# Linear attention, then a GELU network, on one core: the first tile's attention in three units instead of two, and other instructions for r u k and for the state chain

## The chip, the cores and the metric

The kernel runs on one core of one Trainium2 chip. The metric is device microseconds for one execution. Before the change it was 582.84 us, the median of three runs (582.12 to 584.59).

## What is computed

The reference has two stages. Per batch entry and head, a state of 48 x 48 is carried over 768 tokens:

```python
cur = np.einsum('bhd,bhe->bhde', u[None] * kt, vt)
y[:, :, t] = np.einsum('bhd,bhde->bhe', rt, state + cur)
state = wt[:, :, :, None] * state + np.einsum('bhd,bhe->bhde', kt, vt)
```

r, k, v and w are of shape 4 x 8 x 768 x 48. Then y, as x of 3072 tokens by 384, goes through a network of width 2048:

```python
h = x @ w_in
g = 0.5 * h * (1.0 + erf(h * inv_sqrt2))
return (g @ w_out).astype(np.float32)
```

## The kernel before, in words

Tokens are cut into eight tiles of T = 384, two to a batch entry. For each tile there is an `attention` and an `mlp`. The eight heads are four pairs; a pair's two heads lie on the two halves of the 128 partitions. Within a tile tokens stand in chunks of C = 64, two chunks to a block of 128 tokens, so a pair of heads has three blocks (N3) and six chunks (NC).

The attention of a tile goes as follows. `tot` (L508) holds products of w over 2, 4, ... 64 neighbouring tokens. For the first two tiles `halves()` (L567) does, for h = 1, 2, 4, 8, 16, 32, one product d of r and k in each chunk (L550), then multiplies r and k by the decay across half blocks (L592, L603), then copies the part of d that belongs to this h into `a_sb`: by masked copies on VectorE (L615) up to h = 8, by ScalarE (L612) at 16 and 32. At h = 1 the diagonal with u comes too: ScalarE makes r times u (L497), TensorE the product with k, VectorE the masked copy (L563). For later tiles `quarters()` does the same in two levels, and the finest level by sums; it begins with r u k in one VectorE instruction per head pair (L487, four to a tile). Then k is transposed (kt, L787, or moved by DMAs in later tiles), `kv_ps` holds k v of each chunk (L817), `chain_states` (L829, L833) runs state = tot state + kv over the chunks, one `scalar_tensor_tensor` for each head pair and chunk, with kv read where TensorE wrote it, in PSUM. `inside()` (L848) is y from `a_sb`, and L906 adds what the states give. y is copied into `xT`, 384 rows as three groups of 128 (j): ScalarE or VectorE for the rows of the first three pairs (L913, L929), and the fourth pair through `ysb` and six small DMAs (L932, L936).

The network of the first tile is plain (`h_plain` L1114, `g_plain`): for each f of 16 a product over j of `w_in` and 384 columns of xT (L1121), Gelu by ScalarE (L1124), then o = g w_out (L1133). Later tiles do the products with fewer multiplications by sums made on VectorE (`h_ops`, `g_ops`; their products are all recorded at L1043), in an order written out by hand in `ORDER`.

The weights arrive as 64-bit numbers in 16 pieces of 768 KB (eight of w_in, which serve two f each, and eight of w_out). ScalarE (L432, L433, L435) and VectorE (L440, L443) convert each; SP issues the loads (L299, L304).

What fixes the order of instructions is `PLAN`: for each x one string in which each letter advances one generator by one step. For x = 0 the letters are the two units of the first tile's attention ("." for head pairs 0 and 1, "s" for 2 and 3), "f" the next tile's attention, "c" weight conversion, "l" loads, "x" warm products that compute nothing (`keep_warm`, L324; sixteen of them open the kernel, and each product of the first tile's attention but h = 1 has two behind it). For x = 1 and later "." is the network of tile x - 1, "s" the attention of tile x, "f" the beginning of that of tile x + 1. All engines take their instructions in the order so made; a wait holds up all that stands behind it on that engine.

TensorE records two products for each f32 product that the program issues (96 records at L1121 are 48 instructions); transposes of kt record one.

Of the kernel before, what the change touches and what calls it, by code (L numbers as in the profile page):

```python
# [10 lines left out]
F32 = mybir.dt.float32  # L11
# [10 lines left out]
C = 64  # L22
# [18 lines left out]
        ".lls.....sslsc.lsslll.sl.sls..sl.lscsl..sss.lscs.lscs.s.clll.s..s.cccsss...wss..ss.ff"  # L41
    ),
    1: (
        "c.ccc.clccs.cc..csscc...wcsc.csc.s.c.ccsc.scl..c..csclwccs.ccc.sc.cccs..ccs.c..csss.c...s.ccss.scl.l"
        "wccc..ll.csccl.ccclcc.cfc.cwfwf..wcw.sfff...ff.w....lww.fff.fsfx.xfx..w.w.....w.f..f.cw.f..xx.."
    ),
    2: (
        "ss.w.s.sswssw.s.s....s...slsl.s.s.sw..ww.ss.w..sw...sw.ss..w......swws.ss..s.s..s.sss.l.wsw..s..ss.."
        ".s..l....ls.w..sw..s...w.s....ss.ssww.s..w.s...s.s.s..s.sl.s.......s.s.l........s..ls.s......s...l.."
        "f...ls...f..ff....fx.xx....ff.xffx"  # L50
    ),
    3: (
        ".................l...l...ss..s..ss...s.lsss..s..sss.s.s.sss..s..s.s.s......s.ss.ss.ss..s..ss.sss..ss"
        ".ss.s....l.sl..ss.....s.......ss.s.s..ss..s.s.ss..s.s...s......s.s...l....ssss..l..s.s.l..s.ls.f...f"
        "......lfxx.xx..x"
    ),
    4: (
        ".s.ss.l.......s.s............s....sl..s....sssss..s.ss..ss..s..ss......s.s..ssss..ss.sl..s..s..s.s.s"
        "s.s.....s.ss.ssss..ss.s.lss..ss.s..s.....s.s.l.s.s......sss.....ss.....ss..s...s.ssl..s..s...llsls.f"
        "....s.....f.l..fxx.xxx"  # L60
    ),
    5: (
        "...ss..ss.s..ss....s..s................l..ss.l.....s.slss.ss...s.ss.s....ss.s..s...sssss.sss..ss..s."
        "s....s...ssss.sss..s...ssss....s....ssss...s....sls.sssss..s..s........l.....s.....s..ssls..sl..ls.l"
        ".sf....f.f.f...lxxxx.x."
    ),
    6: (
        "...s...s.s.ss.s...s............l.s.....s...ss...ss....s.ss.s..ss..ssslss...s.s...ss.s.s...l.s.sl..ss"
        "s.s...s.s.ss..ss.s.s.sss..s.s...ss..s.ssss..sss...l..s...s.s..ss.s..........s....sl......ss.ls.l.lfs"
        ".s.ff.f....f..l..xx.xfffffffxx"  # L70
    ),
    7: (
        "........................s.s....sssss.s......sss.ss...ss.s...ssss..ss..s.s...ss.ss.....s..s.ss.s..s.s"
        "ss.s...s....s..s......s.s......s.....s..ss.ssss..s.ssss...s........s..s.s.s.s.s....s.......xx....xxx"
# [25 lines left out]
        "E0 e0 A0 a0 C0 c0 F0 B0 A1 b0 a1 E1 B1 F1 f0 e1 f1 k0 G0 G1 b1 g0 D0 A2 d0 a2 C1 l0 B2 g1 i0 c1 E2 e2 F2 "  # L100
        "C2 D1 j0 b2 l1 c2 d1 A3 k1 f2 G2 a3 g2 j1 k2 l2 i1 E3 e3 F3 f3 D2 C3 +22 c3 G3 g3 B3 =a +e5 D3 d2 <i l3 "
        "b3 d3 <g j3 j2 k3 i2 i3 +23 +03 +e0 =i =b +e1 =g =j +01 +e2 =k !b !k !g +e3 !a +E2 +E3 =h !j =c =m !h "
        "+00 =q !m +20 !c <p +E0 +e4 !q =l +E4 =n !l !n =s =p =o !s !p =f =t !f !o =r !t =d =e !r !d !i !e"
    ),
    2: (
        "A0 E0 a0 B0 F0 e0 b0 C0 A1 f0 a1 c0 G0 B1 g0 F1 E1 b1 f1 D0 e1 k0 C1 d0 !i c1 A2 a2 k1 G1 A3 i1 B2 g1 l0 "
        "b2 F2 i0 f2 D1 d1 a3 !b G2 j0 E2 l1 F3 B3 e2 C2 g2 b3 l2 c2 E3 j1 f3 G3 e3 C3 +22 g3 +e5 D2 l3 k2 j3 c3 "
        "d2 D3 i2 d3 =b j2 <g =a <i k3 +03 =g i3 =k =i +e0 +01 +00 +23 !k =j +e1 +e3 +20 !g =h !j +e2 +E3 +E2 =c "
        "!h !d =m +e4 !m !c =q <p +E0 =p =l !p !q =n !l +E4 !n =s !s =f =o !f =t =r !o !t =d =e !r !e !a"
    ),  # L110
    3: (
        "A0 E0 a0 B0 e0 b0 C0 A1 c0 F0 E1 a1 e1 f0 B1 b1 G0 A2 F1 g0 D0 C1 k0 l0 d0 f1 c1 a2 G1 F2 E2 g1 B2 k1 e2 "
        "D1 !a b2 f2 E3 d1 C2 e3 j0 c2 l1 A3 G2 a3 F3 j1 C3 k2 g2 !b i0 f3 D2 l2 d2 G3 g3 i1 D3 c3 k3 B3 <i l3 "
        "+22 d3 j3 b3 i3 j2 <g =i =a =g !d =b +03 =k i2 +23 +e0 +e5 !g +01 +e1 +e2 =j +e3 =h +E3 =c !k !h !j +00 "
        "!i +E2 =m +20 +E0 !m =q =l !q +e4 +E4 !l !c =n =s <p =p !s !p !n =o !o =f =t !f =r =d !t !r =e !e"
    ),
    4: (
        "A0 E0 a0 B0 e0 F0 b0 C0 f0 A1 G0 c0 E1 k0 a1 B1 g0 F1 e1 D0 b1 A2 l0 f1 C1 G1 d0 a2 g1 l1 B2 c1 b2 E2 D1 "
        "e2 F2 A3 f2 C2 j0 j1 d1 c2 a3 k1 k2 G2 F3 g2 i0 E3 f3 D2 i2 B3 e3 G3 l2 i1 g3 D3 d2 C3 b3 +22 <i l3 +e5 "
        "j2 j3 +e2 c3 d3 =i <g =b +03 +23 =g =a =k k3 !g =j +e0 i3 =h !d !k !j +01 !a =c +e1 +E2 +e3 +E3 !i +00 "  # L120
        "!h =m +20 !c !m +e4 =q <p !q =l +E0 !l +E4 =p =n =s !n !p !s =o !o !b =f =d !f =t =r !t !r =e !e"
    ),
    5: (
        "A0 E0 a0 F0 e0 B0 C0 b0 A1 f0 a1 G0 F1 g0 l0 f1 B1 c0 E1 e1 G1 b1 D0 C1 g1 k0 d0 A2 a2 c1 D1 !b E2 d1 B2 "
        "b2 l1 i0 F2 e2 C2 j0 k1 i1 c2 f2 A3 a3 G2 k2 F3 E3 g2 f3 D2 G3 d2 e3 l2 g3 j1 C3 i2 c3 B3 D3 +22 <i l3 "
        "!i k3 d3 =b <g j3 j2 +03 =g b3 +23 =i +e0 i3 !a =a +e5 +01 !g =k =h =j +e1 !k !j +e3 !h =c +e2 +E3 +E2 "
        "=m =q !c +00 !m !d +20 !q =l <p +e4 !l +E0 =p =n +E4 !p =s !n =o !s !o =t =f !f =d !t =r =e !r !e"
    ),
    6: (
        "A0 a0 E0 e0 F0 B0 C0 b0 A1 f0 G0 a1 c0 E1 B1 e1 k0 F1 C1 f1 c1 b1 G1 g0 k1 E2 A2 !a D0 d0 e2 g1 C2 l0 a2 "  # L130
        "c2 D1 d1 B2 A3 l1 b2 a3 F2 E3 f2 F3 !i j1 G2 i1 g2 B3 j0 f3 e3 !d i0 +22 D2 b3 l2 G3 +e5 +e2 k2 !b i2 g3 "
        "C3 D3 c3 l3 j3 d3 d2 <g =a =b j2 =g <i k3 +23 +03 +e0 i3 !g =k +01 =h +00 +E2 !k +e4 =i =c =j +e1 +E4 "
        "+20 !h =q +E0 !j +e3 +E3 !q !c =m !m <p =l =p !l =n =s !p !s !n =o =f !o !f =t !t =r =d =e !r !e"
# [15 lines left out]
def kernel(  # L149
# [72 lines left out]
    def units_of(x):  # L222
        return NPART if x == 0 else 1
# [14 lines left out]
    def load_first():  # L238

        t = bufs[0]  # L240
        loaded[0] = [None, None]
        size = 3 * NP * T // units_of(0)
        order = [(0, 2), (0, 0), (0, 1), (1, 2), (1, 0), (1, 1)]
        for n, (i, part) in enumerate(order):
            s = slice(i * size + part * size // 3, i * size + (part + 1) * size // 3)
            nc.sync.dma_start(out=t[:, s], in_=rkw[0, :, s])
            if n == 0:
                nc.sync.dma_start(out=u_sb, in_=u)
# [14 lines left out]
    def load(x, dma):  # L263

        if x >= NX:
            return
        loaded[x] = [None, None]
        for i in (0, 2, 1):
            t = bufs[x % 2 if i == 0 else 1]
            assert i == 0 or (x - 1, i) in behind, (x, i)  # L270
            for j in range(3):
                a = i * ALL + j * ALL // 3
                dma.dma_start(out=t[:, a:a + ALL // 3], in_=rkw[x, :, a:a + ALL // 3])
                if (i, j) == (1, 2):
                    behind.add((x, "in"))
                yield
        load_v(x, dma)
        yield
# [99 lines left out]
    def make_fine():  # L378
        nc.vector.tensor_tensor(out=fine_mask, in0=s_qs[FINE], in1=t_block, op=ALU.is_equal)
# [68 lines left out]
    def attention(x, unit):  # L448

        first = x % HALVES == 0  # L450
        parts = range(NPART) if units_of(x) == 1 else range(unit, unit + 1)
# [3 lines left out]
        n_u = qs * T  # L455
        base = unit * 3 * n_u
        r, k, w = (bufs[0 if x == 0 or i == 0 and x % 2 == 0 else 1][:, base + i * n_u:base + (i + 1) * n_u]
                   for i in range(3))
        rc, kc = (z.rearrange("p (b i c t) -> p b i c t", b=np_, c=2, t=C) for z in (r, k))
        at = a_sb[:, :, parts[0] * NI:(parts[0] + np_) * NI]  # L460
        st = st_bufs[x % 2]
        before = None if first else st_bufs[(x - 1) % 2]
# [20 lines left out]
        if x >= 2:  # L483
            assert (x - 1, "kx") in behind and (x, "in") in behind
            for q in range(qs):
                m_q = slice(q * T // FINE, (q + 1) * T // FINE)
                nc.vector.scalar_tensor_tensor(out=kx[:, 0:n_u].rearrange("p (a m) -> p m a", a=FINE)[:, m_q],  # L487
                                               in0=r4[:, m_q], scalar=u_sb[:, q:q + 1], in1=k4[:, m_q],
                                               op0=ALU.mult, op1=ALU.mult)
# [3 lines left out]
        else:  # L493

            rus = [kx[:, b * Q * T:(b + 1) * Q * T] for b in parts]
            for q in range(qs):
                nc.scalar.activation(out=rus[q // Q][:, q % Q * T:(q % Q + 1) * T], in_=r[:, q * T:(q + 1) * T], func=AF.Copy,  # L497
                                     scale=u_sb[:, q0 + q:q0 + q + 1])
            rucs = [ru.rearrange("p (i c t) -> p i c t", c=2, t=C) for ru in rus]
# [43 lines left out]
        def products(bs, right, width, rest=False):  # L543
# [10 lines left out]
            if x == 0 and not rest:  # L554
                keep_warm(2)
# [766 lines left out]
```

## Time and profile before

| what | value |
|---|---|
| median of three runs | 582.84 us (582.12 to 584.59) |
| the profiled execution | 583.43 us, its span 581.7 us |
| TensorE busy (PE), weight loads (PEld) | 567.2 us (98%), 510.4 us (88%) |
| VectorE (DVE), ScalarE (ACT) busy | 453.0 us (78%), 290.2 us (50%) |
| warm products, L324 | 46 recorded, 14.7 us |
| first h product, L1121 | starts at 46.26 us |
| first product of the second tile's network | near 125.8 us |
| TensorE clock granted, mean | 0.997 |

The page gives busy time per engine and then the span in 40 equal slices, one digit each, in tenths. A row of the table by stretch reads: the stretch, its length, then busy time and number of instructions of PE, PEld, DVE, ACT and POOL, the granted clock, the share of DMA engines busy and GB/s. The chain of work that ended last is a list of start, length and what it was; "issue" is time in which an engine waited for nothing that the profile shows. A group of instructions reads: line, engine, operation, output<-input, shapes, count, then busy us and mean ns of one, then idle time of the engine just before and who ended it. The mean of one instruction can be longer than its step, since neighbours overlap.

### The profile page before, as it was taken

To read this page: it belongs to the slowest core of one execution; us is meant where nothing else is said; L and a number is where in the kernel's file an instruction comes from. 1 tells how busy PE (TensorE), PEld (TensorE's weight loads), DVE (VectorE), ACT (ScalarE), POOL (GpSimd) and SP (SyncE) were. 2 spreads that over 40 slices of the span, in tenths; PEclk is the share of its full clock that TensorE was granted. 3 is DMA by queue.
4 is the path that set the end of the run, shared out by engine and by line. 5 is a ranking of instruction groups with operands and counts; after the bars stand their busy time and mean duration, and the time that the engine had idled before them with its cause. 6 is when DMAs were issued, how large, how long until landed. Compare 5 with 4: busy or idle time off the path is not lost.

```text
span 581.7 us, 17597 instructions
## 1 busy us (share of the span) xinstructions
PE 567.2 (98%) x7544; PEld 510.4 (88%) x7544; DVE 453.0 (78%) x880; ACT 290.2 (50%) x634; POOL 58.8 (10%) x63
## 2 busy tenths in 40 slices
PE   7789999999999999999999999999999999999997
PEld 3476666669999999999999999999999999999997
DVE  6878967989889978688887979789788988730171
ACT  2468987134762358235672357324671357425520
POOL 3100000003100030003100120003100021002200
PEclk9999999999999999999999999999999999999999
DMA  6669833222451442345223631526314242212401
GB/s 241 200 193 334 275 111 110 70 79 37 68 130 54 112 85 41 95 127 93 29 39 99 171 43 15 126 70 163 43 28 106 94 56 29 43 39 42 54 1 41
DMA packets 61853, 55.07 MB, mean 95 GB/s; under 512 B 32336, under 2 KB 46928, under 8 KB 61776
## 3 DMA queue, kind: packets, MB, share of 16 engines
q1 hardware_dynamic: 50256, 45.62, 26.1%
q0 software_dynamic: 11424, 8.26, 10.9%
q8 instruction: 59, 0.97, 0.7%
q14 instruction: 18, 0.15, 0.1%
q10 hardware_dynamic: 96, 0.07, 0.0%
HBM read 36.24 MB, written 4.72 MB: 70 GB/s over the span
## 4 chain that ended last, share of the span: by engine, by line
PE 94%; DVE 2%; DMA 1%; issue 1%; ACT 0%; SPq 0%; DVEq 0%
PE u_ps L1043 33%; PE h_ps L1043 19%; PE o_ps L1043 13%; PE h_ps L1121 6%; PE o_ps L1133 5%; PE d L689 5%; PE d L550 4%; PE kv_ps L817 2%; PE y_ps L906 2%; PE y_ps L859 2%; DMA rkw<-in_rkw_dram 1%; PE warm L324 1%; DVE st L833 1%; PE d L680 1%; DVE kx L487 1%
## 5 line engine op out<-in xcount | busy, mean ns | idle before, releaser
L1043 PE MATMUL h_ps<-xT,w_in_sb 128*128 128x192 f32 x560 | 109.7, 328 | 0.0
L1081 POOL DMA_DIRECT2D g<-o_sb x42 | 50.8, 1268 | 477.6 <-ACT o_sb L1076 296.9
L1043 PEld LDWEIGHTS h_ps<-xT,w_in_sb 128*128 128x128 f32 x560 | 93.3, 190 | 2.1 <-ACT u_ps L1091 0.8
L1043 PE MATMUL u_ps<-w_out_sb,g 128*128 128x192 f32 x224 | 41.8, 330 | 0.3 <-DVE g L1157 0.3
L1043 PE MATMUL u_ps<-s,w_in_sb 128*128 128x192 f32 x224 | 41.3, 328 | 0.0
L705 ACT COPY a_sb<-d 32x320 f32<-32x320 f32 (+5 forms) x108 | 39.1, 362 | 3.5 <-PE d L689 1.7
L1043 PE MATMUL o_ps<-t,g 128*128 128x192 f32 x224 | 40.0, 326 | 0.0
L1043 PEld LDWEIGHTS u_ps<-w_out_sb,g 128*128 128x128 f32 x224 | 36.7, 190 | 1.0 <-issue 0.5
L1043 PEld LDWEIGHTS u_ps<-s,w_in_sb 128*128 128x128 f32 x224 | 36.9, 190 | 0.6
L1043 PEld LDWEIGHTS o_ps<-t,g 128*128 128x128 f32 x224 | 37.0, 190 | 0.0
L1188 ACT ACTIVATE o_sb<-u_ps 128x192 f32<-128x192 f32 x21 | 6.9, 331 | 57.6 <-PE u_ps L1043 57.5
L833 DVE SCALAR_TENSOR_TENSOR st<-st,tot_sb,kv_ps 128x48 f32<-128x48 f32 x160 | 29.5, 259 | 7.7 <-PE kv_ps L817 7.7
L723 DVE COPY_PREDICATED a_sb<-quarter,d 128x480 f32<-128x480 uint8 (+5 forms) x54 | 23.2, 438 | 13.1 <-PE d L689 12.0
L1121 PE MATMUL h_ps<-xT,w_in_sb 128*128 128x384 f32 x96 | 33.2, 494 | 0.0
L1133 PE MATMUL o_ps<-w_out_sb,g 128*128 128x384 f32 x96 | 31.8, 489 | 0.0
L550 PEld LDWEIGHTS d<-rkw 64*64 64x64 f32 x1152 | 20.2, 140 | 12.9 <-issue 8.3
L1043 PE MATMUL u_ps<-w_extra,g 128*128 128x192 f32 x168 | 30.9, 328 | 0.3 <-ACT u_ps L1167 0.3
L1072 ACT ACTIVATE g<-g 128x384 f32<-128x384 f32 x56 | 28.2, 522 | 5.9 <-DMA g<-o_sb 3.9
L1091 ACT COPY u_ps<-h_ps 128x384 f32<-128x384 f32 x28 | 13.1, 468 | 35.8 <-PE h_ps L1043 25.1
L1157 DVE TENSOR_TENSOR g<-g 128x512 f32<-128x512 f32 x42 | 28.1, 682 | 3.4 <-ACT g L1072 3.1
L689 PE MATMUL d<-kx,rkw 64*64 64x96 f32 x1152 | 29.9, 247 | 0.0
L1083 DVE TENSOR_TENSOR g<-g,o_sb 128x384 f32<-128x384 f32 x14 | 7.5, 548 | 28.4 <-ACT o_sb L1076 28.4
(163 smaller groups left out, 1211.1 us busy)
## 6 DMA issues: line engine op xcount, KB each, us to landing
rkw<-in_rkw_dram SPq DMA_DIRECT2D x54, 256.0 KB, 3.5
g<-o_sb POOLq DMA_DIRECT2D x42, 192.0 KB, 3.6
raw<-in_w_out_dram SPq DMA_DIRECT2D x8, 768.0 KB, 7.7
v_in<-in_v_dram SPq DMA_DIRECT2D x8, 584.0 KB, 4.5
raw<-in_w_in_dram SPq DMA_DIRECT2D x5, 768.0 KB, 5.7
rkw<-kx SPq DMA_DIRECT2D x72, 48.0 KB, 2.0
out_dram<-o_sb SPq DMA_DIRECT2D x17, 192.0 KB, 1.9
rkw<-in_rkw_dram SPq DMA_DIRECT2D x6, 384.0 KB, 3.5
```

What stands on the lines that cost most here:

```text
L550: nc.tensor.matmul(d[half[p], g, n * width:(n + 1) * width], lhsT=kc[half[g], b, i, p], rhs=right(half[g], b, i, p), start=True, stop=True)
L689: nc.tensor.matmul(o[half[p], i * 3 * C // 2:(i + 1) * 3 * C // 2], lhsT=kc[half[g], n // NI, n % NI, p], rhs=rx[half[g], 2 * n + p], star ...
L705: nc.scalar.copy(out=at[z, g, first:behind, (a + 1) * h:], in_=d[z, :, :, to] if g == slice(None) else d[z, :, to])
L723: nc.vector.copy_predicated(out=an[:, :, :, :, (a + 1) * h:], mask=mask.to_broadcast(data.shape), data=data)
L833: nc.vector.scalar_tensor_tensor(out=stq[:, q, c], in0=stq[:, q, c - 1] if c else b4[:, q, NC - 1], scalar=totq[:, q, c:c + 1], in1=kvs[q ...
L1043: nc.tensor.matmul(o, lhsT=lhsT, rhs=rhs, start=start, stop=True, skip_group_check=True)
L1072: nc.scalar.activation(out=g_of(q, a, b), in_=z, func=AF.Gelu)
L1081: nc.gpsimd.dma_start(out=o, in_=z, accum_op=ALU.add)
L1091: nc.scalar.copy(out=u_of[q], in_=a_of[q])
L1121: nc.tensor.matmul(h_ps, lhsT=w_in_sb[:, f // FI, j, f % FI * 128:(f % FI + 1) * 128], rhs=xT[:, j, :], start=(j == 0), stop=(j == NJ - 1))
L1133: nc.tensor.matmul(o, lhsT=gs[f // FG][:, f % FG, i * 128:(i + 1) * 128], rhs=w_out_sb[:, f, :], start=(f == 0), stop=(f == NF - 1))
L1157: (nc.vector.tensor_add if op == "+" else nc.vector.tensor_sub)(*(a(i) for i in (z if z != "E0" else "20", x_, y_)))
```

## The change

The first tile's attention becomes three units: unit 0 is head pairs 0 and 1 on tokens 0 to 255, unit 1 is pairs 2 and 3 on the same tokens, unit 2 is all four pairs on tokens 256 to 383 and goes on from their states. Each has 4 blocks, where the two units of before had 6. The loads of the first tile are cut to match (nine shares of 256 KB where six of 384 KB were), the third unit's shares come later, and unit 2 ("b") stands in the plan of x = 1, beside the first tile's network. There h is done first for 256 columns of xT, two f to a bank and a Gelu of 512 elements, and then for 128 columns, four f to a bank. o is as before.

```diff
-    def units_of(x):
-        return NPART if x == 0 else 1
+    UNITS = ((range(1), 0, 2), (range(1, 2), 0, 2), (range(NPART), 2, N3))
...
-                for f in range(group * FG, (group + 1) * FG):
-                    h_ps = bank("h_ps")[:, 0:T]
...
+            for lo, hi, units in ((0, a, (0, 1)), (a, z, (2,))):
+                assert all((0, "unit", unit) in behind for unit in units)
+                n = hi - lo
+                m = BANK // n
+                for f in range(0, NF, m):
+                    h_ps = bank("h_ps")
+                    for i in range(m):
+                        for j in range(NJ):
+                            nc.tensor.matmul(h_ps[:, i * n:(i + 1) * n], rhs=xT[:, j, lo:hi],
...
+                    nc.scalar.activation(out=gs[f // FG][:, f % FG:f % FG + m, lo:hi], in_=h_ps[:, 0:m * n].rearrange("p (f t) -> p f t", f=m),
+                                         func=AF.Gelu)
```

From the third tile on (x > 1), r u k is r times u on ScalarE, one instruction per head pair, and one product by k on VectorE:

```diff
             for q in range(qs):
                 m_q = slice(q * T // FINE, (q + 1) * T // FINE)
-                nc.vector.scalar_tensor_tensor(out=kx[:, 0:n_u].rearrange("p (a m) -> p m a", a=FINE)[:, m_q],
-                                               in0=r4[:, m_q], scalar=u_sb[:, q:q + 1], in1=k4[:, m_q],
-                                               op0=ALU.mult, op1=ALU.mult)
+                nc.scalar.activation(out=ru[:, m_q], in_=r4[:, m_q], func=AF.Copy, scale=u_sb[:, q:q + 1])
+            yield
+            assert (x, "in") in behind
+            nc.vector.tensor_mul(ru, ru, k4)
```

and the state chain takes all four head pairs at a time, from a copy of kv that ScalarE makes in `kx`, two instructions for a chunk instead of four:

```diff
+        if x > 1:
+            for b in range(np_):
+                kv = kx[:, 0:np_ * 2 * NI * D].rearrange("p (c b z) -> p c b z", c=2, b=np_)
+                nc.scalar.copy(out=kv[:, :, b], in_=kvs[b])
...
+                if x > 1:
+                    old = stq[:, :, c - 1] if c else None if first else b4[:, :, NC - 1]
+                    if old is None:
+                        nc.scalar.copy(out=stq[:, :, c], in_=kv_of[c])
+                        continue
+                    nc.vector.tensor_mul(stq[:, :, c], old, totq[:, :, c:c + 1].to_broadcast([128, qs, D]))
+                    nc.vector.tensor_add(stq[:, :, c], stq[:, :, c], kv_of[c])
```

Two neighbouring half-steps of r in the later tiles (L535, L536) become one instruction. The unit 2 copies into xT go to ScalarE, and its fourth pair's rows take six more DMAs, three of them issued by ScalarE. PLAN is new for every x and ORDER for x = 1 to 6; ORDER[7] stays. In all, TensorE issues 3856 products where 3808 were (48 h products at 256 columns and 48 at 128, for 48 at 384), VectorE 814 instructions where 880 were, ScalarE 692 where 636 were, SP 246 DMAs where 240 were.

## The prediction

> **What bounds the kernel now.** I read the page first, then busy time by stretch of the run, then the chain that ended last over its first 60 us, then the groups with their shapes kept apart. The page's first two parts:
>
> ```profile
> PE 567.2 (98%) x7544; PEld 510.4 (88%) x7544; DVE 453.0 (78%) x880; ACT 290.2 (50%) x634; POOL 58.8 (10%) x63
> ...
> PE   7789999999999999999999999999999999999997
> ...
> DVE  6878967989889978688887979789788988730171
> ```
>
> TensorE is busy nearly always, but its first three slices show 7, 7 and 8 tenths. Busy time by stretch (us; PE, PEld, VectorE, ScalarE, GpSimd; clock; DMA):
>
> ```profile
> 0.00:7.81 7.81, 5.51 (x17) 1.98 (x17) 3.98 (x25) 2.61 (x4) 4.92 (x16) 1.00 0.71 220
> 7.81:46.26 38.45, 31.02 (x1084) 23.16 (x1084) 31.87 (x83) 18.06 (x31) 3.04 (x6) 0.96 0.65 203
> 46.26:90.74 44.48, 44.48 (x781) 29.08 (x780) 34.95 (x45) 41.13 (x58) 0.00 (x0) 1.00 0.72 252
> ...
> 191.50:500.00 308.50, 307.58 (x3816) 295.61 (x3815) 263.43 (x480) 157.79 (x387) 36.20 (x30) 1.00 0.37 80
> ```
>
> From 46.26, where the first h product starts, TensorE does not stop: 0.92 us idle in the 308.5 us of the tiles that repeat. So only two things move the end: TensorE time before 46.26 that does no work of the result, and new waits behind it. Pieces of the chain (start, us, what):
>
> ```profile
> 14.34 0.95 issue
> ...
> 18.75 0.91 issue
> ...
> 23.82 1.21 issue
> ...
> 26.82 1.56 PE d L550 x48
> ...
> 37.67 1.44 issue
> ...
> 44.85 1.40 PE warm L324 x6
> 46.26 1.94 PE h_ps L1121 x6
> 48.19 1.56 PE d L550 x96
> ```
>
> The real work ahead of 46.26 comes from such rates: d 96 records in 1.56 us, 14 products of 48 records are 10.9; kt 1.3, kv 1.5, y 1.6 and 1.3, the second tile's first d 1.6: 18.2 us. The other 28.1 us are idle, warm products, or half speed (x48 once took 1.56). In 7.81 to 46.26 VectorE is busy 31.87 of 38.45 us: it paces the opening, between four "issue" stalls of TensorE.
>
> **The change, part by part,** against the profiled execution: 583.43 us, a span of 581.7 and 1.7 around it. The median shown is 582.84, 0.59 lower; I work out a difference and take it from the median. "Same" below means within 0.5%, 2.9 us, about what a measurement of this kernel tells from no change.
>
> *A, the opening.* A VectorE instruction costs 0.16 us and 1.04 ns an element (L508: 0.944 at 768, 0.560 at 384, 0.357 at 192), so at two thirds of the tokens 0.56 becomes 0.43, and 0.96 becomes 0.69. From 7.81 to the last copy into xT, by the order of instructions: 8 half-steps 0.43, 8 double ones 0.69, masked copies 4 at 0.72 (from 1.00) and 4 at 0.43 (0.57), 2 diagonals 0.74 (1.02), totals 1.5, two weight pieces 3.0, states 2.7 (12 chain steps where 20 were, 0.184 each, and two copies), fences 0.4, copies to xT 1.7: 24.3. The same list of before gives 32.1 and ran from 7.81 to 44.44, 36.6 us with its stalls. 36.6 x 24.3 / 32.1 = 27.7, so h can start at 35.5. Its shares are 256 KB where 384 KB were, but the sixteen warm products hold TensorE until 7.8 in both. Real work ahead of h falls to 12.0 (14 products of 32 records 7.3, kt 0.9, kv and y 2.1, states' product 0.8, the third unit's first two products 1.0). 28.1 - (35.5 - 12.0) = 4.6 us gained. Ends: stalls gone, 32.5 and -7.6; stalls as long as now on less work, 38.5 and -1.6.
>
> *B, h on 256 tokens beside the third unit.* Each group of h (two f, 12 records, 2.62 us) needs one weight piece, converted by ScalarE in 2.83 us (0.92, 1.0, 1.07, overlapping), and a Gelu of 512 (0.59 by 0.481 at 384). From h's start to the third unit's copies into xT ScalarE has six pieces 17.0, six Gelu 3.5, copies of a_sb and kt 2.4, r times u of two tiles 2.9, ysb and xT 1.9, three DMA issues 2.2: 29.9. TensorE has 21.0 of h, 4.3 of the third unit, 3.1 of the second tile: 28.4. So TensorE waits about 1.5 for ScalarE, and 0.6 more where the third unit's last d, k update, kt stand without an h group between: +2.2. The cover is gone where before h had 4.07 us between products (ScalarE 41.13 of 44.48 already). SP's queue adds to it: six writes to xT, which wait for ysb (about 31), now stand ahead of the loads of pieces 4 to 7, 768 KB each, 5.7 us to land. Ends: 0 and +4.6 (each later Gelu a piece behind).
>
> *C, widths and switches.* 96 records of 384 columns (4.07 for 12) become 96 of 256 and 96 of 128. At 0.854 ns a column (11.81 for 36 on o_ps) that is -0.7. Seven more runs of full-array products stand between small ones; after a switch 12 records take 0.13 more than at that rate: +0.9. Sum +0.2. This needs a load of weights hidden behind 128 columns:
>
> ```profile
> L1043 PEld LDWEIGHTS h_ps<-xT,w_in_sb 128*128 128x128 f32 x560 | 93.3, 190 | 2.1 <-ACT u_ps L1091 0.8 <-ACT g L1072 0.5
> ...
> L787 PE MATMUL kt_ps<-ident,rkw 128*128 128x128 f32 x24 | 2.9, 273 | 0.0
> L787 PEld LDWEIGHTS kt_ps<-ident,rkw 128*128 128x128 f32 x24 | 2.7, 141 | 0.5 <-issue 0.2
> ```
>
> kt has just that shape: 128 columns, each with its own full load, 12 in 1.31, 109 ns each, load included; I take it. Far end: 190 ns a record, 96 x 81 ns = +7.8.
>
> *D, the second tile.* In TensorE's order ten 384-column products now stand ahead of the second tile's kv, none before, so kv ends near 93.5 (now 90.7) while the second MLP starts 2.2 earlier, 123.0 for 125.2. VectorE needed 29.7 us from its last state (94.05) to the operands of the third tile's first products (123.72); now 31, with two weight pieces behind it: 97.2 + 31 = 128.2. Sixteen products of 192 columns (0.325 each, 5.2) stand ahead of that use: 128.2. Just in time: +0.8, for I can't place this to a microsecond. Ends 0 and +5.4 (below).
>
> *E, the later tiles.* r u k:
>
> ```profile
> L833 DVE SCALAR_TENSOR_TENSOR st<-st,tot_sb,kv_ps 128x48 f32<-128x48 f32 x160 | 29.5, 259 | 7.7 <-PE kv_ps L817 7.7
> ...
> L487 DVE SCALAR_TENSOR_TENSOR kx<-rkw,u_sb 128x384 f32<-128x384 f32 x12 | 9.2, 892 | 0.0
> ...
> L480 DVE TENSOR_TENSOR kx<-rkw 128x1152 f32<-128x1152 f32 x3 | 6.6, 2203 | 0.0
> ```
>
> Four took 3.06 us. One product of 1536 that strides like L480's (1.74 ns an element) takes 2.9; contiguous 1.76. I take 2.9. The chain: 20 steps at 0.184 are 3.7; ten instructions of 192 elements, each waiting for the last (0.357 and 0.03), 3.9. So VectorE saves nothing much; ScalarE gets four products, two copies out of PSUM and a first state, 3.6 us a tile, at 51% busy. What can gain is that kv's banks come free after two copies: one wait of y for the chain was 0.33. Of 0.92 idle I take -0.4; ends -0.9 and +0.6 (a Gelu late behind the new copies).
>
> [...]
>
> Sum: -4.6 + 2.2 + 0.2 + 0.8 - 0.4 = -1.8: 581.6 on the profiled execution, **581.0** from the median.
>
> **Rivals.** (1) *The opening is kept whole.* B and D are nothing: -4.6 + 0.2 - 0.4 = -4.8, 578.0. For it: TensorE had no wait after 46.26 though ScalarE was 92% busy. Against: B's sums, 29.9 over 28.4. (2) *Slower: VectorE comes late to the second MLP.* D's lag against TensorE is 7.9 us more than now. If products that stand ahead cover 5.2 of it, 2.7 is lost at the first products of the third tile, and 2.7 again where the third MLP needs that tile: 5.4, 585.6; with B at 3.1 instead of 2.2, 586.5. It decides once VectorE's operands are over 5 us behind the second MLP's start. Against: 5.5 us of VectorE idle between 130 and 190. (3) *Loads of weights are not hidden at 128 columns:* 190 ns a record, 581.0 + 7.6 = 588.6. For it is only the 190; against, kt's 109, and that 192 columns step at 162.5 under loads of 190. [...] (4) *The edit on the later tiles does not do what it says:* VectorE saves nothing. That is in my sum.
>
> **How the numbers follow.** Forecast 0.49 (579.9 to 585.5), rival 1 0.37, rival 2 0.10, rival 3 0.04; rival 4 moves none. Faster by over 0.5% (below 579.9) 0.37, within 0.49, slower (over 585.8) 0.14. The range runs from 576.8, most of rival 1 with A's stalls partly gone, to 586.5, which takes in rival 2 and leaves rival 3 out.
>
> **What would show it.** A: the first 256-column h at 35.5, between 32.5 and 38.5. B: ScalarE over 95% busy from there for 30 us, TensorE idle about 2 us, ahead of kt and ahead of the first 128-column h. C: 12 records of 128 columns in 1.31 us. D: the third tile's first d L689 waiting for VectorE near 128. E: PE idle in the repeating tiles below 0.9, r u k still near 2.9 us. I am wrong if h starts after 39, if TensorE waits more than 4 us between there and 130, or if 128 columns take over 130 ns.

## The result, and the profile after

The changed kernel takes **591.75 us** (median of four runs, 590.53 to 593.65), the one before beside it 583.72 us (582.12 to 584.73): 1.0143 times as long, 95% interval 1.0101 to 1.0185. The forecast was 581.0 us, its range 576.8 to 586.5. It was wrong, in sign and in range.

The profiled execution is the slowest of the four, 593.65 us with a span of 591.9; two others, with a mean granted clock of 0.996 instead of 0.991, took 3 us less. The page's lines:

```profile
PE 575.2 (97%) x7640; PEld 524.4 (89%) x7640; DVE 447.1 (76%) x814; ACT 320.5 (54%) x687; POOL 58.9 (10%) x63
...
PE   7989989999999999999999999999999999999997
...
DVE  6885676899998977779796979779795989640171
```

TensorE's row now has 8 tenths in the sixth slice, where before it had 9 in all from the fourth to the last but one. Busy time by stretch (columns as in the prediction), cut at the first h product, where the third unit ends, and at the second tile's network:

```profile
7.80:37.59 29.79, 24.59 (x730) 15.98 (x729) 24.39 (x78) 16.65 (x33) 0.20 (x1) 1.00 0.73 243
37.59:66.01 28.42, 27.87 (x446) 22.56 (x440) 21.08 (x47) 24.32 (x36) 3.00 (x5) 0.94 0.49 182
66.01:134.98 68.97, 65.99 (x1090) 49.48 (x1084) 52.43 (x80) 36.73 (x55) 0.00 (x0) 0.95 0.33 122
```

h starts at 37.59, 8.7 us earlier than the 46.26 of before. But the second tile's network starts at 134.98, where it was 125.84. From there to the end of the span it is 456.9 us now and 455.9 before. So of the 10.2 us between the two profiled executions 9.1 have come up by then: 8.7 us are gained ahead of h, and 17.8 are lost between 37.6 and 135, a stretch of 97.4 us that took 79.6. In it TensorE is idle for 3.5 us and the granted clock is 0.94 and 0.95. The chain of waits shows where (start, us, what):

```profile
70.93 4.32 PE h_ps L1175 x36
75.25 1.53 PE d L567 x96
76.78 2.88 PE h_ps L1175 x24
79.65 0.82 PE d L567 x47
80.48 0.56 issue
81.04 0.95 PE d L567 x49
...
82.02 1.77 DVE rkw L621
...
83.83 1.23 PE d L567 x67
85.06 1.90 issue
86.96 1.07 PE d L567 x29
88.03 5.35 PE h_ps L1175 x24
93.38 1.53 PE d L567 x96
```

Two of the second tile's products stop in the middle, after 47 and after 67 of 96 records, for "issue". Then 24 records of 128 columns take 5.35 us that took 2.88 eleven us before: half speed. The clock by single microseconds (PE busy, clock, DMA share, GB/s):

```profile
85.00:86.00 1.00, 0.06 (x3) 1.00 0.22 83
86.00:87.00 1.00, 0.04 (x4) 0.67 0.09 28
87.00:88.00 1.00, 1.00 (x30) 0.50 0.00 0
```

It falls at 86.35 and stays at 0.50 until 93.17, 6.8 us. A first such spell runs from 38.56 to 41.97, 3.4 us, behind the 1.18 us that TensorE waited for ScalarE just ahead of h; there 12 records of h took 4.47 us for 2.79. Ahead of both stalls loads fill the DMA queues, until about 85. The queues between 80 and 85 us (packets, MB, share of the 16 engines):

```profile
q1 hardware_dynamic: 797, 1.95, 99.3%
q8 instruction: 1, 0.02, 1.4%
```

The second line is the queue that the profile names instruction: one packet of 16 KB beside 797 of the first queue.

The times of these packets in the trace tie them to the stalls. One starts at 78.73 and one at 84.67, and TensorE goes on at 81.04 and 86.96, 2.3 us behind the start in both cases. In the kernel before it goes on 2.4 to 2.5 us behind the start of a packet at each of the four stalls of its opening. What differs is when the packet starts. Counted in steps of 128 records from where TensorE goes on (the last section says why), the two packets start 2.9 us behind the record at 75.78 and 3.6 us behind the one at 81.04. Behind the one at 94.43, with the queues idle, the packet starts 0.7 us later.

The 17.8 us that the stretch is longer, from the rows: 6.8 of work that only moved behind the first h product (third unit 5.3, the second tile's first d 1.5), 1.5 for h in two widths (33.9 for 32.4 at full clock), 0.6 for o in shorter runs, 0.3 for the slower diagonal (the third unit's product with u), 3.5 idle, 4.8 at half clock (1.7 + 2.5 of h, 0.6 of d). Sum 17.5.

### The profile page after: what moved, and what is told of

Its sections match the earlier page's. It is cut to its first block, busy times and chain, and to the rows that moved or that the text cites. A ratio compares the mean times of both kernels' runs of the same rounds, so it can differ in the third digit from the quotient of the medians.

```text
span 591.9 us, 17801 instructions
## 1 busy us (share of the span) xinstructions
PE 575.2 (97%) x7640; PEld 524.4 (89%) x7640; DVE 447.1 (76%) x814; ACT 320.5 (54%) x687; POOL 58.9 (10%) x63
## 3 DMA queue, kind: packets, MB, share of 16 engines
q0 software_dynamic: 11424, 8.26, 10.8%
## 4 chain that ended last, share of the span: by engine, by line
PE 84%; DVE 7%; ACT 4%; issue 3%; ACTq 1%; DMA 1%; DVEq 0%
PE u_ps L1091 28%; PE h_ps L1091 19%; PE o_ps L1091 11%; PE o_ps L1190 5%; PE h_ps L1175 5%; PE d L707 5%; PE d L567 4%; PE kv_ps L837 2%; PE warm L334 2%; ACT kx L504 2%; DVE kx L507 1%; DVE rkw L489 1%; DVE tot_sb L525 1%; ACTq L982 1%; PE y_ps L951 1%
## 5 line engine op out<-in xcount | busy, mean ns | idle before, releaser
L1091 PEld LDWEIGHTS h_ps<-xT,w_in_sb 128*128 128x128 f32 x560 | 93.1, 190 | 4.7 <-DVE xT L1077 2.8
L1175 PE MATMUL h_ps<-xT,w_in_sb 128*128 128x256 f32 (+1 forms) x192 | 38.8, 362 | 0.0
L1175 PEld LDWEIGHTS h_ps<-xT,w_in_sb 128*128 128x128 f32 x192 | 32.1, 213 | 3.1
L1214 DVE TENSOR_TENSOR g<-g 128x512 f32<-128x512 f32 x42 | 28.4, 682 | 2.0 <-ACT g L1120 1.8
L707 PEld LDWEIGHTS d<-kx,rkw 64*64 64x64 f32 x1152 | 24.8, 133 | 4.3 <-issue 3.4
L1091 PEld LDWEIGHTS u_ps<-w_extra,g 128*128 128x128 f32 x168 | 27.8, 190 | 0.6 <-ACT u_ps L1224 0.6
```

What stands on the lines that cost most here:

```text
L707: nc.tensor.matmul(o[half[p], i * 3 * C // 2:(i + 1) * 3 * C // 2], lhsT=kc[half[g], n // NI, n % NI, p], rhs=rx[half[g], 2 * n + p], star ...
L1091: nc.tensor.matmul(o, lhsT=lhsT, rhs=rhs, start=start, stop=True, skip_group_check=True)
L1175: nc.tensor.matmul(h_ps[:, i * n:(i + 1) * n], rhs=xT[:, j, lo:hi], lhsT=w_in_sb[:, (f + i) // FI, j, (f + i) % FI * 128:((f + i) % FI + 1 ...
L1214: (nc.vector.tensor_add if op == "+" else nc.vector.tensor_sub)(*(a(i) for i in (z if z != "E0" else "20", x_, y_)))
```

## The experiments

The table is for reading them: us from the span's start of the first h product and of the second tile's network in each profiled execution, the time between, the rest of the span behind, then the median of the runs and its ratio to the kernel before on the same chip. The first two columns hold to about 0.2 us, since the rows of before and after mix starts by the chain and by the timeline, and the others go by the timeline.

| kernel | first h | 2nd network | between | behind | median | ratio, 95% interval |
|---|---|---|---|---|---|---|
| before | 46.26 | 125.84 | 79.6 | 455.9 | 583.72 | 1 |
| after | 37.59 | 134.98 | 97.4 | 456.9 | 591.75 | 1.0143, 1.0101 to 1.0185 |
| opening only | 38.48 | 131.54 | 93.1 | 456.5 | 591.13 | 1.0131, 1.0109 to 1.0152 |
| second tile later | 36.98 | 129.79 | 92.8 | 458.0 | 589.42 | 1.0091, 1.0066 to 1.0116 |
| less DMA | 37.99 | 128.29 | 90.3 | 457.0 | 587.71 | 1.0081, 1.0054 to 1.0108 |
| second tile later, less DMA | 37.99 | 129.55 | 91.6 | 458.1 | 588.87 | 1.0108, 1.0079 to 1.0136 |
| second tile later, opening only | 37.77 | 130.56 | 92.8 | 458.4 | 589.86 | 1.0120, 1.0094 to 1.0147 |
| three queues | 35.31 | 130.40 | 95.1 | 457.7 | 590.71 | 1.0146, 1.0123 to 1.0168 |
| loads later | 36.29 | 126.49 | 90.2 | 457.1 | 587.12 | 1.0069, 1.0043 to 1.0094 |
| loads later, opening only | 38.35 | 128.53 | 90.2 | 456.8 | 586.88 | 1.0059, 1.0037 to 1.0081 |
| loads later, three queues | 35.94 | 127.24 | 91.3 | 457.6 | 586.77 | 1.0065, 1.0043 to 1.0087 |
| these two and opening only | 36.99 | 127.31 | 90.3 | 456.9 | 586.58 | 1.0067, 1.0046 to 1.0087 |

**Which part.** One kernel has the change's later tiles alone (the last two code fences of the diff in "The change", with the changed plan behind the second tile), the other its opening alone (these undone).

> The kernel of before with the change's instructions for the later tiles alone (r u k by ScalarE and one product, chain over all head pairs, with the changed plan for the tiles behind the second); the opening and the first tile's h are as before. Theory 1 (the loss of 8.0 us lies ahead of the second tile's network): the two traces spend 455.9 and 456.9 us behind that point, so this kernel takes 583 to 585 us, 1.000 to 1.002 of before. Theory 2 (ScalarE's extra 3.6 us a tile and the copies out of PSUM cost a part of the 8 us, in every later tile): 586 us or more.

> The changed kernel with the later tiles' instructions put back to what they were before (and the plan of before from the third network on); the opening in three units and h in two widths stay. Theory 1 (the loss lies in the opening and beside the first tile's network): 590 to 592 us, with the second tile's network starting near 135 as in the changed kernel. Theory 2 (later tiles): 584 to 587 us.

The later tiles alone: 585.5 us, 1.0032 (1.0014 to 1.0050), 1.9 us, between the two expectations. The opening alone: 7.6 us. So theory 1 holds for most of the loss, and theory 2 for a smaller part that I had put at 1 us at most. The two add up to 9.5 us where both together lose 8.3 (5.9 to 10.8), which is no difference. From 200 to 500 us TensorE is idle for 0.92 us before and 1.96 in the kernel with the later tiles alone; in the waits of TensorE behind 125 us these are the longest (us, times, longest):

```profile
PE h_ps L1070 <- DVE xT L1056: 1.0, 3, 0.6
PE y_ps L933 <- issue: 0.7, 1, 0.7
PE h_ps L1070 <- ACT o_sb L1165: 0.4, 1, 0.4
```

VectorE comes late to the sums of x, though it has 8 us less to do (busy for 445.1 us, 453.0 before).

**The later tiles' two edits, each on the plan of before.** The diff of each is its part of the same fences.

> The kernel of before with only r u k done as in the changed kernel (r times u by ScalarE four times a tile, one product by k on VectorE, and the two half-steps of r in one instruction), on the plan of before with one step more, set four letters ahead of the old one in each plan. Both later edits together cost 1.9 us (0.8 to 2.9) on the new plan. Theory 1 (the instructions gain nothing and lose nothing, the loss comes with the new plan, which lets VectorE come late to the sums of x): 1.000 of before within 0.15%, 582 to 584 us. Theory 2 (r u k itself costs, through the wait of VectorE for ScalarE): 1.002 or more, 584.5 us.

> The kernel of before with only the state chain of the later tiles done as in the changed kernel (kv copied by ScalarE into kx, then two VectorE instructions a chunk over all head pairs), on the plan of before, the copies in the step of the kv products. Theory 1 (neutral instructions): 1.000 of before within 0.15%. Theory 2 (the chain costs: its ten instructions wait for each other and for two ScalarE copies, so y starts later): 1.002 or more, 584.5 us. My sum had both edits at -0.4 us.

584.88 us, 1.0035 (1.0016 to 1.0054), and 584.69 us, 1.0033 (1.0015 to 1.0051): theory 2 both times. The two don't add: together, on the new plan, they cost 1.9 us, and each alone on the old plan about as much. The profiled executions are slow ones of their kernels (587.69 and 586.55 us), so the waits below show where time goes, not how much of the median. The longest wait behind the opening, of r u k:

```profile
PE d L691 <- ACT o_sb L1140: 2.1, 1, 2.1
```

It is the third tile's first product, at 130.4. The copy named had ended at 129.64; VectorE's last operand came only at 130.3, for VectorE had stood still for ScalarE's r times u before:

```profile
104.27 2.90 DVE L491 TENSOR_TENSOR kx<-kx,rkw 128x1536 f32<-128x1536 f32 x1 [4.38 <-ACT kx L488]
```

ScalarE came to it at 101.13, directly behind weight conversions; in before VectorE began r u k at 97.09, without a wait. So a part of this price belongs to the place I gave the new step. The longest wait of the chain, at 172.7:

```profile
PE u_ps L1059 <- ACT third_row L1204: 1.2, 1, 1.2
...
171.57 0.64 ACT kx L824
```

Here the new copy of kv stands on ScalarE ahead of two copies that free TensorE's banks (they end at 172.68).

**Two widths.** In the kernel before:

```diff
-                    for j in range(NJ):
-                        nc.tensor.matmul(h_ps, lhsT=..., rhs=xT[:, j, :], start=(j == 0), stop=(j == NJ - 1))
+                    for lo, hi in ((0, 256), (256, T)):
+                        for j in range(NJ):
+                            nc.tensor.matmul(h_ps[:, lo:hi], lhsT=..., rhs=xT[:, j, lo:hi], start=(j == 0), stop=(j == NJ - 1), skip_group_check=True)
```

> The kernel of before, with each h product of 384 columns of the first tile issued as one of 256 and one of 128 columns, in the same order and with the same Gelu; nothing else is changed. Theory 1: only the width costs; the changed kernel's trace shows 0.232 us a record at 256 and 0.120 at 128 where 384 took 0.339, so 96 times 0.013: 1.3 us, 585 us. Rival (loads of weights are not hidden at 128 columns, 190 ns a record as the far end of the prediction had it): 7 us or more, 590 us. My forecast's own value was 0.109 a record: about 0.

583.51 us, 1.0007 (0.9994 to 1.0020). Its chain of waits:

```profile
49.43 6.09 PE h_ps L1122 x36
...
57.05 4.12 PE h_ps L1122 x24
```

Twelve of 256 and twelve of 128 columns take 4.12 us where twelve of 384 took 4.07. A load of weights takes 0.191 us there in the mean, yet a pair of records with its two loads steps on in 0.343 us: the load does not show at 128 columns. 0.4 us in all is the price of the widths, less than the 1.3 expected, and rival 3 is dead. The other 1.1 of h's 1.5 us belong to the shorter runs between small products.

**The second tile later.** In the plan of x = 1 (the letters from the middle on):

```diff
-cscc.scs..scc..sl.ccs.clslcs.s.ssc.wcclslc.lcl.fcscclccsccc.wfl.swc.s.f.s.c.w.wf.bwww.x.f...x..wf..f
+c.ssc.s.cc.ss.sl.cc.ssclc.s.ssc.swccc.sllllcl.sfccclccccc.swfl.wc.s.f.s.sc.w.wf.bwww.x.f...x..wf..f.
```

> The changed kernel with one thing moved in the plan of x = 1: from its level h = 4 on the second tile's attention stands later, its products one or two groups further back among the first tile's h and o products, so that at least 24 records of h or 8 of o (2.8 us) stand between one product and the next; loads and the third tile's first steps that need it follow. Theory 1 (TensorE loses 3.5 us idle near 80 to 87, because only 12 records of 128 columns, 1.5 us, stand in front of a VectorE update of 1.8 us, and then 2.5 us more at half clock): TensorE idle there falls below 1 us, the clock stays up after 87, and the time falls by 3 to 5 us, to 587 to 589. Theory 2 (the stalls named issue, 2.5 of the 3.5 us, belong to the dense run of small products and short h products and not to the order; or VectorE falls behind the second tile's network when this tile comes later): 590 us or more.

589.42 us. The stretch falls from 97.4 to 92.8 us; one stall of 0.84 us is left, and the clock stays at 1.00. Time falls by 0.0052 of before, 3 us (0.2 to 5.9 from the two intervals), as theory 1 had it, at the low end: VectorE gives back 2 of it, 1.1 in a wait of y for it at 112 us and 1.1 behind 130.

**Fewer bytes.** Seven eighths of the bytes of the w_out pieces are left out, and GpSimd writes zeros in their place; in the changed kernel, and then in before as its control:

```diff
+            if i >= len(ins):
+                nc.gpsimd.memset(dst[:, :, DM // 8:].bitcast(F32), 0.0)
+                dst, src = (z[:, :, 0:DM // 8] for z in (dst, src))
             if not gate:
                 nc.sync.dma_start(out=dst, in_=src)
```

> The changed kernel without seven eighths of the bytes of the eight w_out pieces (they are not loaded, and GpSimd writes zeros in their place, so the network's output is wrong; all products, conversions and copies stay). It takes away the transfers that fill the DMA queues between 68 and 85 us, when TensorE twice stopped for 'issue' (0.56 and 1.90 us). Theory 1 (those stalls are TensorE's instructions arriving late: each packet of the queue named instruction is 16 KB, and waits behind weight pieces): the stalls in 75 to 90 fall below 0.3 us, no half clock follows, and the time falls by 2 to 5 us, to 587 to 590. Theory 2 (the stalls belong to TensorE's own sequence of small products): they stay at 1 us or more, and the time stays within 1 us of 591.75.

> Control for the run with fewer bytes of w_out: the kernel of before with the same left out (seven eighths of the bytes of the eight w_out pieces, GpSimd writes zeros in their place; the network's output is wrong). In before no stall named issue stands between 46 and 126 us, so theory 1 (transfers held up TensorE's instructions only in the changed kernel's dense stretch) gives no change: 1.000 of before within 0.15%, 582 to 584 us. If instead all kernels run faster with fewer bytes, it falls by 2 us or more, and the 4 us found there say nothing of the change.

587.71 us: 0.0062 of before less than the changed kernel, 3.6 us (0.7 to 6.5). The control takes 581.97 us, 0.9991 (0.9975 to 1.0007): no change. No issue stall and no half clock is left between 38 us and the second tile's network: what theory 1 foretold.

**All bytes, at another time.** In the plan of x = 1 (one l goes from the line ahead of the one shown, too) and in the third tile's load:

```diff
-cscc.scs..scc..sl.ccs.clslcs.s.ssc.wcclslc.lcl.fcscclccsccc.wfl.swc.s.f.s.c.w.wf.bwww.x.f...x..wf..f
+scc.scs..scc..s.ccs.csllllcs.s.ssc.wcclslc.lcl.fcscclccsccc.wfl.swc.s.f.s.c.w.wf.bwww.x.f...x..wf..f
...
+                if x == 2 and i != 1:
+                    nc.vector.memset(t[:, a:a + 1], 0.0)
                 dma.dma_start(out=t[:, a:a + ALL // 3], in_=rkw[x, :, a:a + ALL // 3])
```

> The changed kernel with all its bytes loaded and the right output, but with the third tile's six loads of r and w (1.5 MB, which stood between the w_out pieces from 68 to 76 us) put behind the second tile's copies at h = 16 and held there by a one-column write of VectorE; the last two w_out pieces stand behind them on SP's queue. The DMA queues were idle from 86 to 102. Theory 1 (it is the traffic between 75 and 85 that holds up TensorE's instructions): the two stalls of 0.56 and 1.90 us go or fall below 0.5 together, no half clock follows, and the time falls by 2 to 4 us, to 587.5 to 590, near the 1.008 of the run with fewer bytes. Theory 2 (fewer bytes helped in another way, or the held loads delay the third tile): 591 us or more, with waits of TensorE or VectorE for loads behind 100 us.

587.12 us, 4.3 us less than the change as it came (1.4 to 7.2), with nothing left out. The timeline shows the same products as the chain above (start, us, and in brackets the idle time ahead):

```profile
74.21 2.94 PE L1177 MATMUL h_ps<-xT,w_in_sb 128*128 128x128 f32 x24
77.08 1.60 PE L569 MATMUL d<-rkw 64*64 64x32 f32 x96
78.61 1.60 PE L1177 MATMUL h_ps<-xT,w_in_sb 128*128 128x128 f32 x12
80.56 1.60 PE L569 MATMUL d<-rkw 64*64 64x32 f32 x96 [0.35 <-DVE rkw L623]
82.10 2.94 PE L1177 MATMUL h_ps<-xT,w_in_sb 128*128 128x128 f32 x24
```

No product is cut in two, 24 records of 128 columns take 2.9 us both times, and what is left is 0.35 us for VectorE. The same work and bytes, and six one-column writes of VectorE: the stalls of 0.56 and 1.90 us went with the large loads beside them, and the 6.8 us of half clock went too. That instructions came late beside the loads is my reading, from the 2.3 us between the start of a packet and the end of each stall. The first spell of half clock stood elsewhere: it followed the 1.18 us of waiting for ScalarE, and in two other profiled executions (second tile later; loads later, opening only) the clock stayed at 1.00 behind the same wait.

**The floor.** Both remedies together, and the later order with the later tiles put back:

> Both remedies on the changed kernel: the second tile's products later (as in the run of that name) and seven eighths of the bytes of w_out left out (the output is wrong, all other work stays). It asks for the floor: what the change costs when neither the stalls nor the short covers are there. Theory 1 (the earlier start gains 8.7 us, of which 7.0 are work that only moves behind it; narrower products, more switches and waits in the later tiles cost 3 to 4): 585 to 587.5 us, 1.003 to 1.007 of before, not faster even so. Theory 2 (stalls and order are all that is wrong with the change): 581 us or less.

> The changed kernel with the second tile's products later (as in the run with that name) and the later tiles' instructions put back to before's: the best that can be made of the opening in three units with what is known so far. If the two add, 591.75 less 2.3 to 3 less 1.9: 586.5 to 587.5 us, 1.005 to 1.008 of before: still slower, since from the first h product on the narrower products, their switches and the third unit's own products take what the earlier start gives. If the opening alone was worth its forecast (4.6 us), it comes out at 583 us or below.

588.87 and 589.86 us, both above what I expected. The stalls can be saved only once, and the later order still costs its 2 us of VectorE (behind: 458.1 and 458.4). Then what sets h's start:

```diff
-                        (nc.scalar if x == 0 and z * NJ + j > 2 else nc.sync).dma_start(out=xT[...], in_=ysb[...])
+                        n = z * NJ + j
+                        dma = nc.sync if x else (nc.scalar if n > 2 else nc.sync) if i0 else (nc.sync, nc.scalar, nc.gpsimd)[n % 3]
+                        dma.dma_start(out=xT[...], in_=ysb[...])
```

> The changed kernel with one edit: the six small DMAs that bring the fourth head pair's rows of tokens 0 to 255 into xT are issued two each by SP, ScalarE and GpSimd, where SP and ScalarE issued three each (3.09 us on ScalarE, from 32.02). Theory 1 (the first h product waits for these rows, issued until 35.1 and landing 1.8 to 3.1 us later, and that is why it came at 37.6 and not at my 35.5): it starts about 1 us earlier, at 36.2 to 36.8, and the time falls by 0.5 to 1.5 us, to 590.3 to 591.3. Theory 2 (VectorE's list or the third unit's diagonal product sets the start): no change, 37.5 and 591.75 within 0.5.

h starts at 35.31, earlier than theory 1 said, and earlier than in any of the eight profiled executions that issue the rows as the change does (36.29 to 38.48); two later kernels with this edit start at 35.94 and 36.99. So the six DMAs have a hand in the start. Whether by landing or by the time that ScalarE spends on issuing them, this run doesn't separate: its share of the issues ends at 32.6 instead of 35.1, and r times u for the third unit's product, which stands ahead of h, comes that much earlier. But the time is 590.71 us, 1.0146: no gain that can be measured; stalls of 1.19 and 1.62 us and half clock stand at 77 to 89 as before. Since they may have swallowed it, three more on the kernel with the loads later:

> The kernel with the third tile's loads later, with the later tiles' instructions put back to before's (and the plan of before from the third network on). Theory 1 (the two parts add once the stalls are gone): 1.0069 less 0.0032, 1.003 to 1.005 of before, 584.5 to 585.5 us. Theory 2 (they do not add: the first of the later tiles needs the cheaper VectorE instructions, since the second tile ends later): 1.006 or more, 586.5 us or more, with TensorE waiting for VectorE ahead of the third tile's products between 126 and 140.

> The kernel with the third tile's loads later, and with the six row writes on three queues, so that h starts near 35.3 instead of 36.3 to 37.6. Theory 1 (step A holds: an earlier start is time as long as nothing later takes it): 1 to 2 us less than 587.12, 585 to 586.3 us, 1.004 to 1.0055. Theory 2 (what follows the first h products is bound by other things, weight conversion or the third unit's VectorE work, and the start does not matter): 587 us within 0.6, 1.0065 to 1.008.

> All three on the changed kernel: the third tile's loads later, the row writes on three queues, the later tiles' instructions as in before. If both parts count: 583 to 584.5 us, 1.000 to 1.003 of before. It is the best case for the split opening; below 1.000 would mean that the split can win, 1.005 or more that neither part counts here.

1.0059, 1.0065 and 1.0067, none apart from 1.0069: by the numbers the less hopeful expectation each time. By the traces the later tiles' old instructions do gain what they cost alone (idle from 200 to 500 us: 1.05 and 1.15 with them in the opening-only kernels, 1.87 and 2.28 in after and loads later), but that is 1 us, inside the intervals. The earlier start is given back in the stretch behind it (91.3 for 90.2: 0.66 us for VectorE's r and k update, 0.51 issue). Nothing here beats the kernel before.

## Why the prediction was wrong

- **A, the opening, -4.6: measured -1.9.** It is this step that failed first. h started at 37.59, inside my 32.5 to 38.5, but 2.1 after my 35.5. I scaled VectorE's list to the last copy into xT; the end is not VectorE's but ScalarE's:

```profile
32.02 3.09 ACTq L982 DMA_DIRECT2D xT<-ysb  x3
...
36.44 1.22 PE L567 MATMUL d<-kx,rkw 64*64 64x64 f32 x32 [1.18 <-ACT kx L515]
```

ysb stands at 32.0. Three DMA issues hold ScalarE until 35.1, its copies into xT and r times u stand behind them, and the product that stands ahead of h waits 1.18 us for r times u. The rows take another 1.8 to 3.1 us to land. The six DMAs are as many for 256 tokens as for 384, and my list of VectorE's work has neither their issue nor their landing. And 6.8 us of work moved, for 6.2: a product of 32 records costs 0.62, more than a third of 1.53.
- **B, +2.2: 0.7.** ScalarE was busy for 24.3 of 28.4 us, not over 95% (its DMA issues, 0.8 us there, are not counted as busy). TensorE waited 0.55 for VectorE and 0.17 for ScalarE.
- **C, +0.2: about +2.1** (1.5 of h, 0.6 of o). The record of 128 columns took 0.120 us, near my 0.109 and far from 0.190: the load did not show in it, as the term took it; the term's size was wrong. The gain by columns, which I put at 0.7 (its rows, 31.5 for 32.4, give 0.9), did not come.
- **D, +0.8: 0 where I put it.** The third tile's first products did not wait for VectorE. The second tile's kv ended at 106.1, not 93.5, behind the stalls. When the order was moved back further, the point of decision of rival 2 did come near: the third tile's first product then waited 0.48 us for VectorE, and the later order cost 2 us in all.
- **E, -0.4: +1.0 by the traces,** +1.9 (0.8 to 2.9) by the runs. r u k took 2.88 us (median of six), as forecast (2.9). ScalarE's added work was not free at 51% busy: VectorE waited 4.5 us for r times u in the changed kernel, in six waits, and TensorE 1.4 us for VectorE's sums of x from the second tile's network on, where before it had no such wait.
- **No term at all: stalls and clock, +7.3.** This is the largest miss. The sum has no term for issue stalls and half clock behind the start of h, and gives no reason for that; in this execution they took 2.5 and 4.8 us, and with the loads moved 4.3 us went by the medians. I had read four "issue" stalls in the opening of before as part of the opening, and did not ask what they were. The rows that would have told were there (the counts of records between them, below).

With 0.3 us for the slower diagonal and 0.3 of waiting for VectorE near 83.5 the measured terms come to 9.8 of the 10.2 us between the two profiled executions.

All three signs that I named for being wrong stayed away: h before 39, waits of 3.5 us under 4, 0.120 under 0.130. A list of signs needs the granted clock and the kinds of waits, not their sum alone. None of the rivals came true; 588.6 of rival 3 is near by accident.

With the loads moved, and so without the stalls, the changed kernel still loses 4.0 us (2.5 to 5.5, from the interval 1.0043 to 1.0094). In that kernel's profile: an earlier start of 10.0 against a stretch longer by 10.6 (6.8 moved, 1.5 h, 0.5 o, 0.3 diagonal, 1.3 waits), and 1.2 behind. The profile's sum is 1.8, and it was the fastest run of its kernel; how the other 2 us divide is open, since the start of h differs by 2 us from one execution to the next (36.3 to 38.5 with the same opening).

## What to carry to other kernels

A stage started earlier gains its idle time less the work that only moves behind the new start (here a start 8.7 us earlier, and 6.8 us of work that moved); count that work from the rows before the gain. Where many small products stood close together here, TensorE stopped for 0.56 and 1.90 us beside large loads, and with the loads moved the time fell by 4.3 us: keep large loads away from such a stretch, and move a load before moving an order. Work given to an engine that is half idle still stands in a queue ahead of what others wait for: ScalarE was busy for 51%, and the later tiles' edits cost 1.9 us.

## What the runs showed of the hardware

In before and after TensorE's stalls named issue of 0.3 us and more (0.31 to 1.90) stand 128 records apart or near a multiple of that; not every 128th record brings one. In after, between the stalls at 80.48 and 85.06, it runs 49 + 12 + 67 = 128 records, each with its load; in before, between 14.34 and 18.75, 39 + 2 + 48 + 2 + 37 = 128, and to 23.82 again 11 + 2 + 48 + 2 + 48 + 2 + 15 = 128; the next stall, at 37.67, comes 381 records on, near three times 128. The queue named instruction brought 60 packets and 0.98 MB in after, 16 KB each, against 2 x 7640 / 60 = 255 records of TensorE to a packet. Counted with their loads, 128 records are 256, about as many as came to a packet. In after such a packet started 2.9 and 3.6 us behind the 128th record beside the large loads, and 0.7 us behind it with the queues idle; with the loads moved the two stalls were gone.

In after the clock fell to half at 38.56, 2.1 us behind the end of a gap of 1.18 us, and at 86.35, within one of 1.90 us, and stayed there for 3.41 and 6.83 us, the second twice the first; in before it did so once, at 26.77, for 3.41. A gap alone does not decide it: in before one of 1.44 us, at 37.67, left the clock at 1.00, and so did gaps of 1.2 us in two other kernels (second tile later; loads later, opening only). What decides it, no run here shows.
